# Linear attention and a gated feed-forward layer on one core: other loads first, two chunks' diagonal by TensorE instead of four, first states scaled by VectorE, a new hand-written order

## The chip, the cores and the metric

The kernel runs on 1 core of one Trainium2 chip. The metric is the device time of one launch in microseconds. Engines are called PE (TensorE matmul), PEld (its weight loads), DVE (VectorE), ACT (ScalarE), POOL (GpSimd) and SP (SyncE, which issues the DMAs).

## The reference

```python
for t in range(S):                       # B=4, H=8, S=768, D=48
    kt, vt, rt = k[:, :, t], v[:, :, t], r[:, :, t]
    cur = einsum('bhd,bhe->bhde', u[None] * kt, vt)
    y[:, :, t] = einsum('bhd,bhde->bhe', rt, state + cur)
    state = w[None, :, :, None] * state + einsum('bhd,bhe->bhde', kt, vt)
x = y as [3072 tokens, 384]
h = x @ w_in                             # 384 -> 2048
g = h * erf(softplus(h))
return g @ w_out                         # 2048 -> 384
```

## The kernel before, in words

**Attention.** The sequence is cut into pieces of 128 tokens: 24 chunks, number g = 4 * piece + batch. A block is one piece of all four batches (chunks 4b to 4b+3, 512 tokens); there are 6 blocks. Heads lie in pairs, 48 + 48 rows of 112. One chunk takes these steps, each a word of the order written out at the end of the file: `La`, `Lb` load its two parts; `K`, `R`, `N` scale k, r and k in the other layout by powers of w; `A` (line 290) makes the 128x128 score matrices of both halves; `P` masks them into `am`; `Y` (313) multiplies with v and adds the state's part; `D` (335) makes the chunk's addition to the state; `Sa`, `Sb` add it, `Sc`, `Sd` scale the state by w to the 128th; `Xa`, `Xb` (356, 359) split y into a high and a low part of the feed-forward input x, in the first block with `Xc` (370), in which PE subtracts the high part in PSUM.

**The diagonal** (the term with u) is made in two ways. In the chunks that have a word `G`, DVE or POOL multiplies r and k (`G`, 224), PE sums the product over the head with two columns (`V`, 232), the sums are scaled onto v (`Q`, `diag_v`, 249) and PE adds them with `ident` (the last twelve matmuls of `Y`). `V` also turns k (238) and `N*` copies it back (255). In all other chunks `Qa`, `Qb`, `Qc` (259, 262, 266) multiply and reduce on DVE or POOL, and `M` (277 or 279) lays the sums on a diagonal, onto which `P` (295) copies the scores. Before, chunks 0 to 3 have `G`.

**Feed-forward.** A step n is one block and one of 16 slices of 128 hidden columns. Steps 0 to 7 are slices 0 to 7 of block 0, steps 8 to 15 the same slices of block 1, steps 16 to 23 slices 8 to 15 of block 0, 24 to 31 those of block 1; from step 32 on block after block. `f` is h = x @ w_in (9 matmuls of 512 columns, line 392), then a chain of nine alternating steps on ACT and DVE (`a b z c d e g h l`), then `p` (9 matmuls, 452) into the accumulators. `O` stores: partial sums after steps 7 and 15, results at a block's end.

**Weights** arrive as 64-bit numbers in 16 groups of 768 columns: `F0g` loads group g of w_in, `F1g` of w_out (two buffers), and `C0g`, `C1g` turn each into a high and a low part in six steps a to f: a (ACT, 123), b, c, d (DVE, 125, 127, 130), e (ACT, 133), f (DVE or, with a +, POOL, 135). There is one work buffer `wt`, so a group's step a waits for step f of the group before. Group g of w_in is needed by the steps of slices 2g and 2g+1: `f8` and its block need none that steps 0 to 7 did not, `f16` is the first that needs group C04, and `p20`, `p22` need C16 and C17.

**What sets the order.** Every engine works its own list in the order of the words of `ORDER`, and waits where an operand isn't there yet. A + behind a word puts it on POOL, a * on ACT, else DVE. `W n` puts n dummy matmuls (92) at that place, after 16 at the start. SP issues the loads in the same order; chunks other than 3 share three buffers.

Of the kernel before, what the change touches and what calls it, by code (L numbers as in the profile page):

```python
# [685 lines left out]
C01f W2 f2 N5+ S4a l0 f3 L6a F02 L6b C11a d1 C11b C11c e1 a2 C11d P51 p0x p0y Q7b+ b2 z2 g1 Q7c C11e a3 b3 z3 S4b h1
l1 C11f+ Q6a+ p0z Y5 p1 D5 C02a C02b C02c C02d Q6b Q6c c2 d2 c3 d3 X5a C02e e3 C02f f4 M60+ R6+ K6+ M61+ M70+ M71+ K7+
g3 h3 S5b X5b l3 e2 S5a g2 F13 L8a F12 a4 b4 z4 h2 l2 f5 a5 b5 z5 A6 c4 C13a c5 d5 d4 P60 P61 C13b C13c C13d f6 e5 a6
p2 A7 C13e b6 g5 e4 h5 P70 N7+ C13f+ N6+ C12a p3 P71 Y7 z6 g4 l5 h4 c6 d6 X7a f7 Y6 C12b C12c C12d X7b l4 C12e D6 C12f
p4 a7 F06 L8b b7 z7 e6 X6a c7 C06a d7 X6b f8 D7 g6 C06b C06c p5 h6 C06d Q8a S7b l6 a8 b8 C06e e7 Q8b+ z8 g7 c8 F05 L9a  # L690
# [5 lines left out]
C07d g15 z16 P80 P81 p14 C07e F17 O71b O72b a17 c16 b17 z17 h15 l15 C07f+ N8+ p15x p15y p15z Y8 D8 C05a C05b C05c C05d
c17 d16 d17 e16 e17 C05e O150a g16 h16 g17 C05f f18 l16 f19 p16x O150b C17a O151a h17 O152a a18 b18 C17b C17c C17d z18
C17e c18 l17 C17f d18 e18 O151b F15 C15a O230a O152b L10a O231a L10b F16 p16y p16z f20 g18 h18 C15b l18 a19 b19 a20
C15c z19 C15d b20 z20 c19 d19 C15e e19 C15f g19 f21 a21 p17 b21 z21 h19 l19 C16a c20 d20 e20 C16b C16c g20 C16d p18
p19 f22 c21 h20 d21 l20 e21 C16e g21 C16f a22 b22 z22 h21 c22 d22 e22 X8a l21 S8a X8b f23 a23 b23 g22 Q10a z23 p20 h22  # L700
c23 d23 e23 l22 S8b Q10b Q10c S8d+ R10+ g23 f24 a24 M100+ p21 h23 A9 f25 P90 P91 l23 a25 b25 b24 z25 N9 z24 K10+ c25
d25 e25 c24 d24 S7c+ M101 p22 p23x p23y p23z A10 f26 O230b g25 e24 h25 P100 N10+ g24 h24 a26 Y9 X9a b26 M110+ l25 P101
l24 z26 f27 a27 p24x c26 f28 a28 b28 d26 e26 b27 O231b K11 S6c+ R11 X9b M111 A11 p24y O230c O232a O232b P110 z28 g26
P111 p24z p25 Y11 D11 c28 h26 l26 z27 c27 X11a d27 e27 g27 X11b h27 S11a l27 f29 p26 d28 a29 b29 e28 L12a O231c L12b
z29 S11b g28 c29 d29 h28 Q12a+ Q12b+ S8c+ l28 f30 a30 b30 e29 g29 z30 Q12c M120 Y10 D10 p27 p28 f31 O310a L13a O232c
# [96 lines left out]
```

## Time and profile before

| | |
|---|---|
| three runs | 538.97, 539.66 (median), 540.29 us |
| the profiled execution | 540.45 us, its span 538.6 us |
| PE busy | 518.6 us, 96% of the span |
| ACT, DVE, POOL busy | 393.0 (73%), 354.4 (66%), 126.2 us (23%) |
| chain that ended last | PE 82%, DVE 6%, DMA 4%, ACT 3% |

How to read it: the span is the time between the first and the last instruction on the core, the execution's own time is 1.85 us longer. PE is busy nearly throughout, but a busy PE is not always at full rate: its clock is granted at one of two levels, and the page shows the granted share in 40 slices. A stretch in which PE is busy with dummies, at the lower clock, or waits, is the only place where the time of a fixed amount of matrix work can shrink. The last matmul starts at 532.03 us; what follows is copies and the output's DMA.

### The profile page before, as it was taken

The page shows a single profiled execution, that of the slowest core. Times are in us where ns is not written, and L with a number is a line of the kernel's source. Part 1 is how long each engine was busy: PE and PEld are TensorE (multiplying, and loading weights), DVE is VectorE, ACT ScalarE, POOL GpSimd, SP SyncE. Part 2 cuts the span into 40 slices and gives each one's busy share as a digit, 9 for nine tenths or more (in the row PEclk, how much of TensorE's full clock was granted, in tenths as well). Part 3 has the DMA queues.
Part 4 walks back from the last instruction along what each step waited for, and adds up shares of the span by engine and source line. Part 5 has one row for each costly group of instructions (what it writes and reads, how often), then busy time and mean ns, then how long its engine had stood idle before and what let it go on. Part 6 is the DMA issues. An engine that isn't in the chain of part 4 may idle for free.

```text
span 538.6 us, 9791 instructions
## 1 busy us (share of the span) xinstructions
PE 518.6 (96%) x3893; PEld 409.5 (76%) x3894; DVE 354.4 (66%) x573; ACT 393.0 (73%) x721; POOL 126.2 (23%) x125
## 2 busy tenths in 40 slices
...
PEclk9599999999999999999999999999999999999998
...
GB/s 280 80 271 162 194 108 182 179 112 60 163 236 1 39 105 127 60 211 1 0 1 53 226 1 0 86 1 59 193 106 86 0 1 2 1 60 0 1 1 64
DMA packets 13988, 47.29 MB, mean 88 GB/s; under 512 B 1776, under 2 KB 2416, under 8 KB 13936
## 3 DMA queue, kind: packets, MB, share of 16 engines
...
## 4 chain that ended last, share of the span: by engine, by line
PE 82%; DVE 6%; DMA 4%; ACT 3%; issue 2%; SPq 1%; DVEq 0%; ACTq 0%
PE acc L452 35%; PE h L392 34%; PE y L313 6%; PE A L290 4%; DMA raw<-in_win_dram 3%; PE ds L335 1%; DMA raw<-in_wout_dram 1%; DVE wt L127 1%; ACT wt L123 1%; DVE s L408 1%; DVE wt L125 1%; DVE h L424 1%; DVE wil L135 0%; ACT gh L430 0%; PE y L370 0%
## 5 line engine op out<-in xcount | busy, mean ns | idle before, releaser
L392 PE MATMUL h<-x,wih 128*128 128x512 f32 x576 | 184.2, 401 | 3.1 <-ACT wih L133 2.0
L392 PEld LDWEIGHTS h<-x,wih 128*128 128x128 f32 x576 | 106.5, 188 | 31.4 <-DVE gl L435 3.4
L452 PE MATMUL acc<-gh,woh 128*128 128x512 f32 x288 | 116.4, 404 | 0.0
L452 PE MATMUL acc<-gl,woh 128*128 128x512 f32 x288 | 114.3, 397 | 1.9 <-DVE gl L435 1.9
L392 PE MATMUL h<-x,wil 128*128 128x512 f32 x288 | 114.3, 397 | 0.3 <-DVE wil L135 0.3
L452 PE MATMUL acc<-gh,wol 128*128 128x512 f32 x288 | 114.1, 396 | 0.0
L424 DVE SCALAR_TENSOR_TENSOR h<-s,h 128x512 f32<-128x512 f32 x96 | 66.4, 692 | 63.7 <-ACT s L420 63.5
L408 DVE SCALAR_TENSOR_TENSOR s<-s,h 128x512 f32<-128x512 f32 x96 | 65.5, 682 | 40.6 <-ACT s L403 40.2
L435 DVE TENSOR_TENSOR gl<-h,gh 128x512 fp32r<-128x512 f32 x96 | 66.1, 688 | 35.6 <-ACT gh L430 33.9
L430 ACT CAST gh<-h 128x512 fp32r<-128x512 f32 x96 | 55.9, 582 | 38.1 <-DVE h L424 28.6
L412 ACT ACTIVATE s<-s 128x512 f32<-128x512 f32 x96 | 60.3, 628 | 26.1 <-DVE s L408 26.0
L399 ACT ACTIVATE s<-h 128x512 f32<-128x512 f32 x96 | 56.9, 593 | 27.8 <-PE h L392 27.6
L452 PEld LDWEIGHTS acc<-gh,woh 128*128 128x128 f32 x288 | 54.2, 188 | 15.0 <-issue 1.0
L452 PEld LDWEIGHTS acc<-gl,woh 128*128 128x128 f32 x288 | 54.3, 188 | 14.8 <-DVE gl L435 2.5
L392 PEld LDWEIGHTS h<-x,wil 128*128 128x128 f32 x288 | 54.2, 188 | 14.1 <-DVE wil L135 1.0
L452 PEld LDWEIGHTS acc<-gh,wol 128*128 128x128 f32 x288 | 54.2, 188 | 13.0
L403 ACT ACTIVATE s<-s 128x512 f32<-128x512 f32 x96 | 60.4, 630 | 1.8
L416 ACT ACTIVATE s<-s 128x512 f32<-128x512 f32 x96 | 60.3, 630 | 1.9
L420 ACT ACTIVATE s<-s 128x512 f32<-128x512 f32 x96 | 60.2, 629 | 1.5
L259 POOL TENSOR_TENSOR att<-att,ub 128x384 f32<-128x384 f32 x14 | 16.7, 1190 | 105.1 <-DMA att<-in_att_dram 65.7
L290 PEld LDWEIGHTS A<-att 48*128 48x128 f32 x384 | 24.5, 193 | 10.2 <-issue 6.3
L295 DVE COPY_PREDICATED am<-mask,A 128x512 f32<-128x512 uint32 x40 | 28.1, 736 | 5.7 <-PE A L290 5.7
...
## 6 DMA issues: line engine op xcount, KB each, us to landing
...
```

The costliest lines, as they stand in the source:

```text
L290: nc.tensor.matmul(out=ap[hh][:, p, :], lhsT=t[r, 512 + p * C:512 + (p + 1) * C], rhs=t[r, p * C:(p + 1) * C], start=True, stop=True)
L392: nc.tensor.matmul(out=h, lhsT=w[:, f, q, :], rhs=x[:, xi, q, :], start=k == 0, stop=k == 8)
L399: nc.scalar.activation(out=s1, in_=e["h"], func=AF.Tanh, bias=FB0, scale=FA0)
L403: nc.scalar.activation(out=s1, in_=s1, func=AF.Tanh, bias=FB1, scale=FA1)
L408: nc.vector.scalar_tensor_tensor(out=e["s"], in0=e["s1"], scalar=FG, in1=e["h"], op0=ALU.mult, op1=ALU.add)
L412: nc.scalar.activation(out=s, in_=s, func=AF.Tanh, bias=FB2, scale=FA2)
L416: nc.scalar.activation(out=s, in_=s, func=AF.Square, bias=FB3, scale=FA3)
L420: nc.scalar.activation(out=s, in_=s, func=AF.Square, bias=FB4, scale=FA4)
L424: nc.vector.scalar_tensor_tensor(out=h, in0=ff[n]["s"], scalar=FC, in1=h, op0=ALU.subtract, op1=ALU.mult, reverse0=True)
L430: nc.scalar.copy(out=e["gh"], in_=e["h"])
L435: eng.tensor_tensor(out=e["gl"], in0=e["h"], in1=e["gh"].bitcast(F32), op=ALU.subtract)
L452: nc.tensor.matmul(out=acc[e], lhsT=w[:, f, es], rhs=g, start=first and i == 0, stop=last and i == 2)
```

## The change

- `G2`, `V2`, `Q2` and `G3`, `V3`, `Q3` are gone: chunks 2 and 3 take the other way to the diagonal (`Qa` to `Qc`, `M`, `P` by copy_predicated), and load their second parts whole (608 KB instead of 224 KB each). Their `N` is a product on DVE instead of a turn on PE and a copy on ACT.
- In the four chunks of the first block the scaling of the state by w to the 128th, which the turn of k by `w128` gave, is a DVE product `Sc`, `Sd` (one for each half, 8 in all) instead of an ACT copy. The table `w128` and its POOL product are gone; for chunks 0 and 1 the turn is a plain transpose.
- The last block's copies of accumulators 1 and 2: each whole, by DVE and by ACT, instead of half and half.
- A new `ORDER`, with dummies as nine pairs (18 after the 16 at the start, before 20).

```diff
-    w128 = fp.tile([PR, NPAIR, PR], F32, tag="o", name="w128")
     def diagonals():
         nc.scalar.mul(out=neg, in_=ident, mul=-1.0)
-        nc.gpsimd.tensor_tensor(out=w128, in0=ident[:PR, None, :PR].to_broadcast([PR, NPAIR, PR]),
-                                in1=wp[:, 7, 0, :, None].to_broadcast([PR, NPAIR, PR]), op=ALU.mult)
...
                 kp = chunks[g][:PR, 512 + p * C:512 + (p + 1) * C]
-                if g < 4:
-                    nc.tensor.matmul(out=kt[:, p, :], lhsT=kp, rhs=w128[:, p, :], start=True, stop=True)
-                else:
-                    nc.tensor.transpose(out=kt[:, p, :], in_=kp, identity=ident[:PR, :PR])
+                nc.tensor.transpose(out=kt[:, p, :], in_=kp, identity=ident[:PR, :PR])
...
         if g < 4:
-            nc.scalar.copy(out=sv, in_=ds[r])
+            nc.vector.tensor_tensor(out=sv, in0=ds[r], in1=w128, op=ALU.mult)
...
-            elif b == NB - 1 and e > 0:
-                nc.vector.tensor_copy(out=o[:, 0:TB // 2], in_=full[n, e][:, 0:TB // 2])
-                nc.scalar.copy(out=o[:, TB // 2:TB], in_=full[n, e][:, TB // 2:TB])
+            elif b == NB - 1 and e == 1:
+                nc.vector.tensor_copy(out=o, in_=full[n, e])
...
 ORDER = """
-L1a L1b U0 L0a L2a L0b F00 L3a F03 L3b L2b B0* C00a B0 H0 K1 R0 K0 R1 T0 W5 A0 G0 V0 G1 C00b P00 P01 R3+ V1 C00c R2 Q0
...
+L0a W2 W2 W2 L1a U0 L0b L2a L2b L3a L3b L1b F00 B0 B0* F01 K0 R0 A0 K1 G0 R1 V0 A1 G1 P00 K2+ V1 Q0 P01 P10 T0 H0 N0*
...
```

The weight groups are turned in the order C00, C03, C10, C01, C11, C02, C13, C12, C06, C14, C04, C07, C05, C17, C15, C16 before, and C00, C01, C10, C02, C11, C03, C12, C13, C14, C05, C04, C07, C15, C06, C16, C17 now. Step f of nine groups is POOL's now (C00, C10, C02, C03, C14, C05, C07, C15, C06), before of four (C11, C13, C04, C07). The order of the loads at the start, SP, before (att_160 is chunk 1, att_164 chunk 0, att_166 and att_171 chunks 2 and 3; 128x1024 is the first part, `raw` is weights):

```order
L68 DMA att_160<-in_att_dram 128x1024
L72 DMA att_160<-in_att_dram 128x448
L81 DMA ub<-in_u_dram 128x384
L68 DMA att_164<-in_att_dram 128x1024
L68 DMA att_166<-in_att_dram 128x1024
L72 DMA att_164<-in_att_dram 128x448
L107 DMA raw_169<-in_win_dram 128x768
L68 DMA att_171<-in_att_dram 128x1024
L107 DMA raw_173<-in_win_dram 128x768
L72 DMA att_171<-in_att_dram 128x448
L72 DMA att_166<-in_att_dram 128x448
```

And now (att_159 and att_170 are chunks 0 and 1, att_174 and att_177 chunks 2 and 3):

```order
L68 DMA att_159<-in_att_dram 128x1024
L68 DMA att_170<-in_att_dram 128x1024
L81 DMA ub<-in_u_dram 128x384
L72 DMA att_159<-in_att_dram 128x448
L68 DMA att_174<-in_att_dram 128x1024
L72 DMA att_174<-in_att_dram 128x1216
L68 DMA att_177<-in_att_dram 128x1024
L72 DMA att_177<-in_att_dram 128x1216
L72 DMA att_170<-in_att_dram 128x448
L107 DMA raw_181<-in_win_dram 128x768
L107 DMA raw_187<-in_win_dram 128x768
```

Chunk 0 comes first instead of fourth, and the first weights come last instead of seventh.

DVE in the first block, before, from the first masks of the scores on (kt holds the sums of `V`, wt the weights in work):

```order
L299 TENSOR_TENSOR am_1_224<-A_1_201,mask 128x512
L127 SCALAR_TENSOR_TENSOR wt_179<-raw_169,wt_179 128x768
L215 TENSOR_TENSOR att_166<-att_166,wr 112x512
L249 TENSOR_TENSOR att_164<-att_164,kt_211 128x4x48 x2
L249 TENSOR_TENSOR att_160<-att_160,kt_227 128x4x48 x2
L130 SCALAR_TENSOR_TENSOR wt_179<-raw_169,wt_179 128x768
L299 TENSOR_TENSOR am_0_311<-A_0_256,mask 128x512
L299 TENSOR_TENSOR am_1_313<-A_1_257,mask 128x512
```

And now (its line 253 is 259 of before, 256 is 262, 260 is 266, 293 is 299, 243 is 249, and 341 the new product of the state):

```order
L212 TENSOR_TENSOR att_174<-att_174,wr 112x512
L256 TENSOR_TENSOR att_174<-att_174 128x384
L253 TENSOR_TENSOR att_177<-att_177,ub 128x384
L260 TENSOR_REDUCE q_307<-att_174 128x8
L293 TENSOR_TENSOR am_1_309<-A_1_214,mask 128x512
L243 TENSOR_TENSOR att_170<-att_170,kt_227 128x4x48 x2
L341 TENSOR_TENSOR sbd<-ds_283,wp 48x4x48
L260 TENSOR_REDUCE q_321<-att_177 128x8
L341 TENSOR_TENSOR sbd<-ds_292,wp 48x4x48 x2
L125 TENSOR_SCALAR wt_352<-wt_352 128x768
L216 TENSOR_TENSOR att_177<-att_177,wkn 128x384
L127 SCALAR_TENSOR_TENSOR wt_352<-raw_181,wt_352 128x768
```

The first group's steps stand among the first masks before, and now behind the masks of chunks 0 and 1 and the first two states.

PE from the end of the dummies to the first `Y`, before, without the rows that repeat:

```order
L290 MATMUL A_1_201<-att_164 128x128
L232 MATMUL kt_211<-uw,att_164 128x2 x4
L238 MATMUL kt_211<-w_134,att_164 128x112 x4
L232 MATMUL kt_227<-uw,att_160 128x2 x4
L238 MATMUL kt_227<-w_134,att_160 128x112 x4
L335 MATMUL ds_247<-att_164 48x48 x8
L290 MATMUL A_0_256<-att_160 128x128
L313 MATMUL y_266<-am_0_222,att_164 32x128 x2
```

And now (284 is 290 of before, 229 is 232, 234 is 238, 307 is 313):

```order
L284 MATMUL A_1_192<-att_159 128x128
L229 MATMUL kt_204<-uw,att_159 128x2 x4
L234 MATMUL kt_204<-ident,att_159 128x112 x4
L284 MATMUL A_0_213<-att_170 128x128
L229 MATMUL kt_227<-uw,att_170 128x2 x4
L234 MATMUL kt_227<-ident,att_170 128x112 x4
L192 MATMUL tp<-ident,wk 128x112 x4
L307 MATMUL y_254<-am_0_224,att_159 32x128 x2
```

The first `A` and `V` follow one another as before, but the two `V` are apart, and the first `Y` comes ahead of the first `D`.

## Rows read from the trace of the kernel before

**Rows 1.** The page: its first line, its line of busy times, and of its 40 equal slices the granted TensorE clock in tenths of full speed.

```profile
span 538.6 us, 9791 instructions
PE 518.6 (96%) x3893; PEld 409.5 (76%) x3894; DVE 354.4 (66%) x573; ACT 393.0 (73%) x721; POOL 126.2 (23%) x125
PEclk9599999999999999999999999999999999999998
```

**Rows 2.** The busy time of each engine in four stretches: from the first `f` on, from the end of PE's last early wait to `f8`, from `f8` to the last weight group, and from there to the last matmul (columns: the stretch, its length, then for PE, PEld, DVE, ACT and POOL the busy us with the count of instructions, then the granted clock, the DMA engines' busy share, and GB/s).

```profile
45.20:74.50 29.30, 25.14 (x240) 17.80 (x239) 27.26 (x40) 21.51 (x39) 14.99 (x10) 1.00 0.48 161
74.50:94.00 19.50, 19.50 (x215) 15.25 (x216) 17.10 (x26) 16.27 (x29) 9.23 (x8) 1.00 0.38 128
94.00:165.00 71.00, 70.14 (x384) 55.16 (x383) 60.38 (x87) 64.41 (x110) 23.12 (x20) 1.00 0.42 143
165.00:532.40 367.40, 365.07 (x2592) 289.82 (x2590) 218.79 (x358) 274.90 (x507) 65.36 (x67) 1.00 0.15 52
```

**Rows 3.** What PE's matmuls waited for in the whole span (us in total, times, longest).

```profile
PE h L392 <- ACT wih L133: 2.0, 1, 2.0
PE acc L452 <- DVE gl L435: 1.9, 1, 1.9
```

**Rows 4.** PE in order of time (start us, us, engine, line, operation, tiles, count; in brackets the idle time before it and what ended it): dummies, the first `A`, the first `Y`, the `Y` behind the second pause, the starts of `f0`, `f8`, `p20` and `p22`.

```profile
7.79 1.24 PE L92 MATMUL dummy<-warm 128*128 128x512 bf16 x5
10.84 1.16 PE L290 MATMUL A<-att 48*128 48x128 f32 x16 [1.80 <-DVE att L211]
22.51 1.93 PE L313 MATMUL y<-am,att 128*32 128x128 f32 x32
39.34 1.65 PE L313 MATMUL y<-am,att 128*32 128x128 f32 x26 [1.97 <-DVE am L299]
45.16 0.73 PE L392 MATMUL h<-x,wih 128*128 128x512 f32 x2
93.99 0.63 PE L392 MATMUL h<-x,wih 128*128 128x512 f32 x2
165.23 0.39 PE L452 MATMUL acc<-gh,woh 128*128 128x512 f32 x1
174.97 0.39 PE L452 MATMUL acc<-gh,woh 128*128 128x512 f32 x1
```

**Rows 5.** Three stretches with the granted clock, columns as in rows 2: the first stretch at the lower level, the second, and a pause of PE.

```profile
12.20:25.60 13.40, 13.20 (x120) 12.09 (x120) 8.84 (x13) 3.52 (x9) 6.17 (x4) 0.50 0.29 117
39.40:42.80 3.40, 3.40 (x54) 2.97 (x55) 3.40 (x7) 2.52 (x9) 0.00 (x0) 0.51 0.90 304
69.30:71.20 1.90, 0.00 (x0) 0.00 (x0) 1.86 (x3) 1.34 (x4) 0.22 (x1) 1.00 0.40 60
```

**Rows 6.** The first loads, columns as in rows 2: from 2 us to the arrival of chunk 0, from there to that of the first weights, and the rest.

```profile
2.00:9.40 7.40, 6.67 (x25) 2.63 (x24) 5.11 (x25) 1.02 (x4) 2.90 (x4) 1.00 0.88 287
9.40:13.30 3.90, 2.33 (x22) 2.17 (x22) 3.10 (x5) 0.03 (x1) 0.00 (x0) 0.85 1.03 406
13.30:16.70 3.40, 3.40 (x18) 3.40 (x17) 2.51 (x4) 1.49 (x4) 2.03 (x2) 0.50 0.79 316
```

**Rows 7.** DVE, POOL and ACT in order of time, columns as in rows 4: DVE's first products of a chunk, a product and two small products while POOL works, one of 384 columns, POOL's two products, ACT's first step a.

```profile
7.33 0.69 DVE L211 TENSOR_TENSOR att<-att,wk 112x512 f32<-112x512 f32 x1
9.49 0.69 DVE L215 TENSOR_TENSOR att<-att,wr 112x512 f32<-112x512 f32 x1 [1.47 <-DMA att<-in_att_dram]
10.10 0.68 DVE L211 TENSOR_TENSOR att<-att,wk 112x512 f32<-112x512 f32 x1
16.73 1.76 DVE L215 TENSOR_TENSOR att<-att,wr 112x512 f32<-112x512 f32 x1
18.41 0.60 DVE L249 TENSOR_TENSOR att<-att,kt 128x192 f32<-128x192 f32 x2
44.31 0.55 DVE L259 TENSOR_TENSOR att<-att,ub 128x384 f32<-128x384 f32 x1
15.90 3.71 POOL L211 TENSOR_TENSOR att<-att,wk 112x512 f32<-112x512 f32 x2
13.27 0.89 ACT L123 ACTIVATE wt<-raw 128x768 f32<-128x768 f32 x1 [6.77 <-DMA raw<-in_win_dram]
```

**Rows 8.** Weight groups, columns as in rows 4: step f of C00, step a of C10, step f of C12 and of C16, the last group.

```profile
28.10 0.95 DVE L135 TENSOR_TENSOR wil<-wt,wih 128x768 fp32r<-128x768 f32 x1
42.90 0.91 ACT L123 ACTIVATE wt<-raw 128x768 f32<-128x768 f32 x1
90.66 0.95 DVE L135 TENSOR_TENSOR wol<-wt,woh 128x768 fp32r<-128x768 f32 x1
164.13 0.96 DVE L135 TENSOR_TENSOR wol<-wt,woh 128x768 fp32r<-128x768 f32 x1
```

**Rows 9.** Step f of the weights by DVE and by POOL (groups of instructions: line, engine, operation, tiles, shapes, count, busy us, mean ns, idle time before and what ended it).

```profile
L135 DVE TENSOR_TENSOR wil<-wt,wih 128x768 fp32r<-128x768 f32 x6 | 6.2, 1026 | 0.0
L135 POOL TENSOR_TENSOR wil<-wt,wih 128x768 fp32r<-128x768 f32 x2 | 3.7, 1871 | 10.5 <-ACT wih L133 10.5
```

**Rows 10.** The last copies (accumulator 0's by ACT at 531.06), columns as in rows 4.

```profile
532.46 0.42 DVE L472 COPY o<-acc 128x256 f32<-128x256 f32 x1 [0.28 <-PE acc L452]
531.06 0.59 ACT L475 COPY o<-acc 128x512 f32<-128x512 f32 x1 [2.21 <-PE acc L452]
532.92 0.37 ACT L473 COPY o<-acc 128x256 f32<-128x256 f32 x1 [0.33 <-DVE o L472]
```

More of the change, by code (lines that the diff above doesn't have):

```diff
@@ L686 @@
[L686 to L690, printed above, removed]
@@ L696 @@
[L696 to L700, printed above, removed]
@@ L701 @@
[L701 to L705, printed above, removed]
@@ new lines @@
+C00c W2 X0c C00d N2 K3 X0b X1a C00e M31* D3 A2 X1c A3 X1b P20 P21 Y2 S3c P30 P31 L5a F10 D2 Y3 C00f+ Q4a+ C01a X2a K4
+C01b Q4b C01c K5 C01d S3d Q4c S2d R4+ X3a X2c X3c W2 X2b X3b f0 f1 C01e L6a L5b F02 a0 b0 C01f R5 M40 M41+ A4 S2c z0
+C10a a1 b1 C10b Q5a z1 C10c C10d c0 d0 e0 c1 d1 C10e f2 W2 a2 W2 W2 W2 F11 L6b P40 g0 h0 b2 Q5b+ C10f+ Q5c P41 l0 C02a
+M50* N4+ z2 M51 A5 C02b C02c C02d K6+ c2 f3 d2 a3 e2 e1 C02e p0x p0y p0z P50 g2 h2 b3 Q6a P51 g1 z3 C02f+ Q6b+ R6+ Y4
+X4a D4 h1 c3 X4b l2 Q6c l1 C11a d3 L7a L7b F03 Y5 f4 f5 M60* X5a M61* e3 C11b C11c N5 C11d S4b S4a X5b C11e F12 R7+
@@ new lines @@
+p8z p9 f12 g10 h10 S7a S6a z11 C05b C05c c11 d11 e11 C05d C05e g11 h11 l10 l11 S7b O72b L10a L10b L9a L9b F07 a12 b12
+C05f+ S6b z12 f13 f14 p10 C04a C04b C04c C04d p11 Y8 c12 a13 b13 d12 F15 e12 g12 z13 a14 C04e C04f b14 z14 h12 l12
+C07a f15 p12 c14 c13 d13 e13 d14 C07b C07c C07d g13 C07e h13 e14 a15 Q10a+ Q10b C07f+ F06 l13 g14 b15 z15 h14 l14 C15a
+C15b f16 f17 c15 a16 d15 p13 p14 b16 S5c C15c C15d z16 e15 a17 g15 c16 b17 z17 h15 l15 C15e d16 e16 Q9a+ g16 C15f+
+Q9b+ c17 d17 h16 l16 p15x O150a p15y f18 e17 C06a f19 O151a a18 b18 a19 p15z p16x O150b F16 p16y g17 h17 b19 O152a
@@ new lines @@
+C06b Q9c C06c C06d z18 l17 z19 D8 p16z p17 C06e c18 d18 e18 c19 g18 Q10c d19 h18 l18 e19 O152b O151b F17 O230a O231a
+L11a L11b g19 S8a M90+ C06f+ S5d+ K9+ R10+ f20 f21 a20 h19 l19 f22 b20 z20 C16a p18 c20 d20 e20 a21 a22 b21 p19 C16b
+S8b C16c C16d g20 z21 b22 z22 h20 l20 c21 C16e d21 C16f e21 C17a g21 h21 C17b l21 f23 p20 a23 b23 c22 d22 C17c z23 e22
+c23 p21 f24 g22 h22 d23 C17d l22 e23 g23 C17e C17f h23 l23 a24 b24 X8a z24 R9 X8b S8d+ M91 N9+ M100+ S7c+ S7d+ Q11a+
+Q11b+ N11+ f25 p22 p23x O230b a25 c24 d24 b25 e24 p23y A9 f26 O230c O232a z25 g24 h24 l24 c25 d25 a26 b26 P90 f27 P91
@@ new lines @@
+O231b Y9 z26 K10 Q11c M101+ p23z p24x p24y c26 d26 X9a e26 M110* M111+ S6d+ R11+ S8c+ K11+ S6c+ X9b g26 h26 e25 O232b
+l26 A10 g25 P100 P101 p24z h25 l25 a27 f28 b27 z27 A11 p25 f29 c27 d27 e27 a28 b28 P110 P111 Y11 D11 z28 g27 c28 d28
+h27 l27 a29 X11a e28 b29 g28 S11a X11b p26 f30 h28 z29 l28 c29 d29 e29 a30 b30 S11b z30 f31 a31 c30 Y10 D9 p27 O231c
+O232c L12a L12b O310a O311a L13a L13b d30 b31 e30 p28 R12 g29 g30 h30 X10a Q12a+ Q12b+ l30 X10b h29 S9a l29 z31 f32
+p29 f33 a32 b32 z32 c31 c32 d31 Q12c e31 M120* K12+ S9b Q13a+ g31 h31 M121 A12 N12 S11d+ K13+ S11c+ Q13b+ S9c+ p30 d32
@@ new lines @@
+l31 e32 g32 h32 a33 b33 p31x O310b Q13c M130+ N10+ l32 p31y f34 f35 P120 P121 z33 O311b Y12 D10 p31z p32x a34 b34 c33
+z34 a35 c34 d33 e33 g33 d34 h33 b35 O310c O312a O312b l33 z35 p32y p32z e34 c35 X12a g34 d35 e35 h34 p33 f36 g35 h35
+l34 S10b l35 a36 b36 z36 S10a O311c L14a f37 c36 a37 p34 D12 f38 p35 L14b L15a O312c L15b b37 d36 S12a z37 Q14a+ e36
+c37 Q14b+ g36 h36 a38 X12b S12b l36 b38 d37 e37 g37 z38 h37 c38 l37 Q14c f39 p36 f40 a39 d38 e38 g38 h38 N13+ R13+
+N14+ M131* b39 l38 z39 A13 p37 a40 c39 b40 d39 e39 Q15a+ Q15b+ S9d+ P130 P131 z40 g39 c40 h39 l39 f41 d40 p38 p39 f42
@@ new lines @@
+K17+ S15d+ f49 p46 p47x p47y p47z A16 f50 a49 b49 z49 c48 d48 e48 S14c+ g48 Q18a K18 c49 h48 d49 l48 f51 e49 O470a
+L17b O470b g49 h49 O471a a50 b50 Q17a R17+ P160 l49 z50 a51 c50 d50 O472a f52 p48x p48y p48z b51 Q17b Q17c S12c z51
+P161 e50 c51 g50 h50 l50 Q18b Q18c M170* N18 N17 M171+ p49 A17 a52 d51 e51 b52 g51 z52 h51 P170 l51 p50 f53 a53 b53
+c52 d52 P171 z53 Y16 Y17 p51 f54 c53 e52 g52 d53 h52 e53 M180+ R18+ M181* g53 l52 h53 l53 a54 X16a X17a b54 X17b X16b
+z54 p52 f55 f56 A18 p53 c54 d54 e54 g54 h54 l54 a56 a55 b55 b56 z55 z56 P180 N16+ S14d+ p54 D16 f57 c55 c56 d56 e56
@@ new lines @@
+S16b g56 P181 Y18 d55 e55 S16a g55 h55 l55 a57 h56 b57 l56 z57 D18 f58 f59 p55 X18a c57 d57 a58 e57 b58 S18b O472b
+O471b L19a L19b X18b K19 g57 z58 c58 d58 h57 S18a l57 p56 p57 e58 g58 a59 h58 b59 Q19a+ R19+ l58 Q19b z59 Q19c c59 d59
+M190+ e59 M191+ f60 A19 f61 g59 P190 P191 Y19 N19 D19 h59 a60 b60 z60 l59 p58 f62 c60 a61 d60 e60 X19a b61 z61 g60
+X19b h60 c61 d61 l60 L20a L20b D17 L22a a62 b62 z62 e61 g61 Q20a p59 f63 h61 c62 Q20b+ l61 d62 a63 b63 e62 p60 L22b
+L21a L21b p61 f64 K21 S19b S16d+ S19d+ K22 g62 h62 S19a z63 Q20c M200+ K20+ c63 d63 l62 S17a e63 a64 b64 S17b g63 h63
```

74 lines of the change are left out of this document (27 added, 47 removed).

## The prediction, made before the changed kernel was run

> **What bounds the kernel now.** I read the page first: the span, and PE busy for 96% of it [rows 1]. That says that PE's list is the path, and that only three things can be gained: time in which PE waits, time in which it runs dummies, and time at the lower clock. So I looked for them by stretch. From 165 us to the last matmul PE is busy for 365.07 of 367.40 us, from 74.5 to 165 for all but 0.9 [rows 2]; the list of what PE waited for holds one wait of 1.9 us behind 94 us and else only early ones [rows 3]. What can be gained lies in the first 94 us. PE's rows there show it: first `Y` at 22.51, `f0` at 45.16, `f8` only at 93.99 [rows 4], and the granted clock was at its lower level, 1.2 GHz, from 12.2 to 25.6 us and again for 3.4 us, with PE busy, after pauses of PE of 1.80 and 1.97 us (they stand in brackets, and ended at 10.84 and 39.34) [rows 4, 5].
>
> Why PE pauses after `f0`: the weight groups pass one work buffer, one behind the other. From the end of C00's step f (28.10 + 0.95 = 29.05) to the end of C16's, the last, (165.09) 15 groups took 136.0 us, 9.07 each; the six from C10 to C12 took 48.7, 8.1 each [rows 8]. `p20`, which needs C16, started at 165.23 [rows 4], just behind it. So two chains matter up to `p22`: PE's list, and the weight groups.
>
> **The change, part by part.**
>
> *First loads.* Chunk 0 was fourth in the queue, 1.47 MB with what stands ahead of it, and DVE had it at 9.49; by 9.4 us 7.4 x 287 GB/s = 2.12 MB had moved. The first weights end at 3.01 MB in the queue and came at 13.27, when 3.7 MB had moved [rows 6, 7]. A load thus lands when some 0.65 to 0.7 MB more have moved than lie up to its end. Now chunk 0 is first and takes the place of the load that was there by 7.33 without a wait. Chunk 1 (1.05 MB) lands by some 8.0, chunk 3's second part (3.77 MB) at 15.1, F00 (4.78 MB, 5.48 to be moved: 13.3 + 1.77 MB / 406 GB/s) at 17.7 instead of 13.27. Chunks 2 and 3 bring 0.79 MB more, some 2 us at that rate, all of it ahead of F00. That is the price of the new order of loads, and it falls on weights.
>
> *PE's start.* 22 dummies, one more than now but with no transposes between them, end as now at about 7.79 + 1.24 = 9.0 [rows 4]; `K0` and `R0` need two steps of 0.61 from 7.33 [rows 7], 8.55. `A0` follows at 9.0 without the pause of 1.80. I take it that the clock then stays up, since what brought it down here followed a pause. `A0`, `V0`, `A1`, `V1` and the transposes (1.1 + 1.6 + 1.1 + 1.6 + 0.6) end at 15.0; `Y0` starts there, 7.5 earlier.
>
> *DVE in the first block.* Gone are two `G` on DVE or POOL, four small `Q`, eight ACT copies of states; new are six steps of 384 columns, two of them on POOL, two `N` on DVE, eight state products of 0.3, the `M` on POOL and ACT. Up to C00's step b the list holds 11 steps of 512 columns at 0.61, 4 of 384 at 0.48, 8 small ones at 0.30 [rows 7]: 11.0 us, from 7.33 to 18.3, with waits for chunk 3's load 19.2. Steps b, c, d with one `N` between end at 22.2, e at 23.0, f by POOL 1.87 [rows 9] at 24.9. The rest of the block on DVE (`N2`, `K3`, four `P`, one S) ends at 26.4; with `Y3`, two `Xc` and the last copies `f0` starts at about 29 instead of 45.2. PE loses some 7 us of `V` and ident work, part of it at the lower clock; it is part of these 16 us and isn't counted again.
>
> *Where these 16 us go.* Not all reach the end, since the weight chain sets `p22`. C00 is done at 24.9 instead of 29.05, but it is followed by C01 at once, where before C10 started only at 42.90 behind C03. Six groups more, with C12 the last of them, at 48.7: 73.6. Behind it DVE has C13's three steps and two z before the last part of x for block 1 (4.2), so `f8` is at 78 to 79, 15 earlier. From `f8` to `p22` PE has one `p` and one `A` less and one `D` more (2.8 us less than the 81.0 of now), so PE alone would reach `p22` at 157. The chain needs 24.9 + 136.0 = 161, since C17 is again the fifteenth group behind C00 and the DVE work up to there is the same within 1.1 us. I take 161, the later. Before it was 174.97 [rows 4]. PE waits some 4 us in between.
>
> *The rest.* Behind `p22` PE has 357.45 us up to 532.42, and in the new order one `A` more, 1.2. The waits of 1.9 and 0.4 may go or others come; I leave them. In the tail, accumulator 2's copy is 0.42 + 0.04 + 0.37 on two engines one after the other [rows 10], now one on ACT like accumulator 0's, 0.59 [rows 10]: 0.24 less. The other half copy runs beside matmuls and counts nothing.
>
> *Sum.* 161 + 357.45 + 1.2 + 6.18 - 0.24 = 525.6 of span against 538.6 [rows 1]. The execution took 1.85 more than its span, and stood 0.8 above the median of the runs: **about 526.6 us**, 13 less.
>
> *Bounds.* Below: DVE's list alone sets `f8`. Counted with its rows' durations it has 64.1 us of work up to there, behind 7.2 of tables: 71.3. If PE then never waits, `p22` is at 149.5 (78.2 later), and with the wait of 1.9 gone the time is 513. Above: five more groups have step f on POOL, 1.87 instead of 1.03 [rows 9], 4.2 in all, and the low clock of rows 5 comes back (next part), 6.7: 538. I take the measured pace, since as many DVE steps stand between the groups as before.
>
> *A rule against it.* DVE's product of 512 columns at 16.73 took 1.76 instead of 0.69, while POOL ran two products; the small ones that read PSUM took 0.30 as ever [rows 7]. The Trainium skill (SBUF — State Buffer, "SBUF: two separate sides") says why: DVE with two operands in SBUF and POOL take one port pair in turn, for a whole instruction. The trace agrees. By the rule each microsecond that the new order gives POOL may be taken from DVE: POOL has 30.8 us up to `f8`, counted with its rows' durations, and 28.1 before. If all 2.7 were lost by DVE, the sum would be 529.3 instead of 526.6.
>
> **Rivals.**
>
> *The clock falls again in the new start.* For it: from 12.2 to 25.6 PE was busy for 13.20 of 13.40 us and stayed at the lower level all the same, with `V` and `A`, which the new start has too [rows 5]; against it: from 25.6 to 39 it ran the same kinds of work at the upper level. Price: half of 13.4, 6.7 us on the way to `f0` and C00's steps, which wait for the first states: 533. The Trainium skill (TensorE: Matmul & The Clock Gate, "What's actually happening") has the lower level as the default, which activity releases; by that the pauses between weight groups could bring it back too. The pause at 69.3 to 71.2, 1.9 us long, did not [rows 5].
>
> *The gain at the start is taken back by the weights.* If ACT or POOL makes the groups slower than 9.07, it is lost. ACT is busy for 64.41 of 71.0 us from `f8` to C16 [rows 2]; by the same counting the new order has 78.7 us of ACT work from `f8` to `p22`, in a stretch that I make 82 long. At 10.0 us a group C17 ends at 175 and nothing is won: 540. That is no change.
>
> *Slower.* The same chain, past that point: with 10.4 us a group C17 ends at 181, `p22` waits for it, and the time is 546. It decides from 10.0 on. For it: POOL has nine steps f instead of four, three of them while DVE has the most to do, and later loads of weights wait for buffers in one queue behind loads of chunks. Against it: no stretch of 15 groups was above 9.1 here.
>
> *The order doesn't do what it says.* F00 could land later than 17.7, if the larger chunk loads take more than their bytes. Each microsecond there moves C00, not the first block: 2 to 3 at the most, 529.
>
> **How the numbers follow.** A measurement of this kernel can tell some 0.2%, 1.1 us, from no change. My forecast, a gain of 9 to 14 us or more with the chain at its old pace, has 0.62; the clock 0.14; late loads 0.06; a partial loss to no change 0.10, of which 0.04 within 1.1 us; slower 0.08. Faster by over 0.2%: 0.62 + 0.14 + 0.06 + 0.06 = 0.88; within: 0.04; slower: 0.08. The range reaches from the lower bound to the case in which nothing is won: 513 to 540.
>
> **What would show it.** Right: first `Y` near 15, `f0` near 29, C00's f near 25, `f8` near 79, `p22` near 161, granted clock at the upper level from 5 us on, PE dense behind `p22`. Wrong: a granted clock of 0.5 before `f0`; groups above 9.5 us; new waits of PE behind 165 us above 3 us in sum; a wait for loads of `raw`.

## The result and the profile of the changed kernel

The changed kernel took 525.79 us (median of 4 runs, 524.04 to 527.54), the kernel before 539.97 (4 runs, 538.97 to 541.41): ratio 0.9735, 95% interval 0.9695 to 0.9775. A later repeat gave 526.5 (6 runs, 523.78 to 528.94), ratio 0.9765 (0.9733 to 0.9797). The prediction was 526.6.

The profiled execution took 524.04 us, the shortest of its four; traces are therefore compared span with span: 538.6 and 522.3, 16.3 us apart. That is 2.1 more than the 14.2 between the medians; the account below is one of these two executions. The page, as [rows 1]:

```profile
span 522.3 us, 9636 instructions
PE 506.9 (97%) x3804; PEld 398.0 (76%) x3804; DVE 352.5 (67%) x572; ACT 393.0 (75%) x720; POOL 142.7 (27%) x135
PEclk9998999999999999999999999999999999999999
```

PE is busy for 11.7 us less and does nothing for 4.6 us less; work at the lower clock counts as busy for as long as it takes. The places on PE's list, as [rows 4]; line 284 is 290 of before, 307 is 313, 386 is 392, 446 is 452:

```profile
2.37 7.12 PE L92 MATMUL dummy<-warm 128*128 128x512 bf16 x22 [2.37 <-ACT warm L86]
9.42 1.16 PE L284 MATMUL A<-att 48*128 48x128 f32 x16
14.84 1.08 PE L307 MATMUL y<-am,att 128*32 128x128 f32 x32
28.35 0.97 PE L386 MATMUL h<-x,wih 128*128 128x512 f32 x2
41.19 1.16 PE L284 MATMUL A<-att 48*128 48x128 f32 x14 [1.20 <-DVE am L289]
77.35 0.51 PE L446 MATMUL acc<-gh,wol 128*128 128x512 f32 x1 [0.75 <-DVE wol L135]
81.20 0.77 PE L386 MATMUL h<-x,wih 128*128 128x512 f32 x2
158.07 0.39 PE L446 MATMUL acc<-gh,woh 128*128 128x512 f32 x1
516.14 0.39 PE L446 MATMUL acc<-gh,wol 128*128 128x512 f32 x1
```

The first `A` has no pause ahead of it, `f0` starts at 28.35 instead of 45.16, `f8` at 81.20 instead of 93.99, `p22` at 158.07 instead of 174.97, the last matmul at 516.14 instead of 532.03. The stretches between them (columns as in [rows 2]):

```profile
20.00:28.35 8.35, 7.95 (x146) 6.50 (x145) 8.28 (x15) 5.55 (x13) 5.40 (x3) 1.00 0.78 268
28.35:43.00 14.65, 12.66 (x72) 8.46 (x71) 14.47 (x24) 11.31 (x19) 7.90 (x6) 1.00 0.54 188
43.00:46.80 3.80, 3.80 (x12) 2.97 (x11) 3.73 (x5) 2.80 (x7) 1.22 (x1) 0.55 0.23 92
47.00:81.20 34.20, 31.95 (x375) 24.82 (x374) 33.48 (x47) 27.34 (x54) 20.39 (x15) 1.00 0.45 161
81.20:158.00 76.80, 76.80 (x427) 60.69 (x426) 65.86 (x96) 72.21 (x125) 31.04 (x24) 1.00 0.41 145
158.00:516.60 358.60, 356.61 (x2555) 283.07 (x2554) 210.36 (x343) 265.43 (x486) 68.01 (x70) 1.00 0.15 53
```

Read DVE's column, the third behind the length: from 20 us to `f8` it is busy for 98 to 99% of every stretch. In the kernel before it was not, ahead of `f0`:

```profile
20.00:45.16 25.16, 23.19 (x395) 20.26 (x391) 16.43 (x25) 11.02 (x29) 4.14 (x4) 0.82 0.59 202
45.16:94.00 48.84, 44.67 (x454) 33.09 (x454) 44.40 (x65) 37.83 (x68) 24.21 (x17) 1.00 0.44 148
```

So the account of the 16.3 us is: `f0` 16.81 earlier; 52.85 us from `f0` to `f8` instead of 48.83, 4.02 given back (some 2.8 of it, by estimate, one `p` and one `A` less a `D`, which before stood behind `f8`); from `f8` to the last matmul 434.94 instead of 438.04, 3.10 gained, most of it that same work; behind it 6.16 instead of 6.57, 0.41 gained.

On PE's side the 16.81 us up to `f0` are 24.90 us of busy time instead of 38.69 and 3.45 idle instead of 6.47. Of the 13.8 less busy some 8.3 are, by estimate, the clock: before, 16.6 us of PE's work there ran at half rate [rows 5], and in this execution none did. The rest is matmuls that are gone or stand elsewhere.

The last copies, as [rows 10]:

```profile
515.86 0.69 DVE L465 COPY o<-acc 128x512 f32<-128x512 f32 x1 [2.20 <-PE acc L446]
516.57 0.58 ACT L467 COPY o<-acc 128x512 f32<-128x512 f32 x1 [0.82 <-PE acc L446]
```

The last one ends 0.62 us behind the last matmul (516.53) instead of 0.87.

### The profile page after: what moved, and what is told of

The parts are those of the page before. It is cut to its first block, busy times and chain, and to the rows that moved or that the text cites. A ratio compares the mean times of both kernels' runs of the same rounds, so it can differ in the third digit from the quotient of the medians.

```text
span 522.3 us, 9636 instructions
## 1 busy us (share of the span) xinstructions
PE 506.9 (97%) x3804; PEld 398.0 (76%) x3804; DVE 352.5 (67%) x572; ACT 393.0 (75%) x720; POOL 142.7 (27%) x135
## 4 chain that ended last, share of the span: by engine, by line
PE 87%; DVE 9%; issue 1%; ACT 1%; POOL 0%; DVEq 0%; ACTq 0%; POOLq 0%
PE acc L446 38%; PE h L386 36%; PE y L307 6%; PE A L284 4%; PE ds L329 1%; PE dummy L92 1%; DVE wt L127 1%; DVE am L289 1%; DVE wt L130 1%; DVE wol L135 1%; DVE wt L125 1%; DVE gl L429 1%; DVE s L402 0%; DVE q L260 0%; DVE att L212 0%
## 5 line engine op out<-in xcount | busy, mean ns | idle before, releaser
L273 POOL TENSOR_TENSOR am<-ident,q 128x512 f32<-128x512 f32 x24 | 27.8, 1166 | 96.2 <-DVE q L260 48.4
L289 DVE COPY_PREDICATED am<-mask,A 128x512 f32<-128x512 uint32 x44 | 31.0, 733 | 2.0 <-PE A L284 1.9
```

## The experiments

Starts of `f0` and `f8` and the span belong to the profiled execution, the time is the median of all runs, the ratio is to the kernel before on the same chip.

| kernel | `f0` | `f8` | span | span less `f0` | time | ratio, 95% interval |
|---|---|---|---|---|---|---|
| before | 45.16 | 93.99 | 538.6 | 493.4 | 539.97 | |
| changed | 28.35 | 81.20 | 522.3 | 494.0 | 525.79 | 0.9735 (0.9695 to 0.9775) |
| changed, again | 28.30 | 81.16 | 522.1 | 493.8 | 526.50 | 0.9765 (0.9733 to 0.9797) |
| old, chunk 0 first | 44.23 | 91.94 | 538.5 | 494.3 | 539.11 | 0.9994 (0.9966 to 1.0022) |
| the same, dummies in the pause | 43.80 | 91.59 | 537.3 | 493.5 | 538.18 | 0.9965 (0.9947 to 0.9984) |
| new, chunk 1 first | 33.83 | 87.81 | 529.0 | 495.2 | 532.10 | 0.9881 (0.9846 to 0.9916) |
| new, diagonal by PE, first places | 38.29 | 90.81 | 532.1 | 493.8 | 534.73 | 0.9921 (0.9902 to 0.9940) |
| new, diagonal by PE, better places | 31.76 | 84.54 | 525.6 | 493.8 | 529.09 | 0.9831 (0.9788 to 0.9874) |
| new, three parts undone | 37.07 | 89.48 | 532.1 | 495.0 | 534.64 | 0.9925 (0.9897 to 0.9954) |
| new, without seven steps c | 30.58 | 78.92 | 519.9 | 489.3 | 519.68 | 0.9636 (0.9619 to 0.9653) |
| new, two work buffers | 31.28 | 85.90 | 527.2 | 495.9 | 527.75 | 0.9766 (0.9730 to 0.9802) |
| new, f of C11, C12 by POOL | 31.26 | 82.23 | 525.6 | 494.3 | 526.50 | 0.9757 (0.9729 to 0.9785) |
| the same, Xb first | 28.41 | 80.42 | 526.7 | 498.3 | 530.53 | 0.9810 (0.9780 to 0.9840) |
| new, 16 dummies | 29.33 | 83.52 | 524.5 | 495.2 | 525.52 | 0.9719 (0.9689 to 0.9748) |

The column of the span less `f0` is the finding: where only the start was altered it stays between 493.4 and 495.2 us, old order or new. Whatever `f0` gains or loses arrives at the end, within these 1.8 us.

**The first load alone, in the old order.**

```diff
-L1a L1b U0 L0a L2a L0b F00 ... H0 K1 R0 K0 R1 T0 W5 A0
+L0a L1a U0 L0b L2a L1b F00 ... H0 K0 R0 K1 R1 T0 W5 A0
```

> The kernel before, with one thing changed: chunk 0's two parts are loaded ahead of chunk 1's, and DVE scales k and r of chunk 0 first. The rest of the old order stays. Theory (the gain of the change starts with the first load, and what follows PE's first pause is the low clock): the first A starts at 9 to 9.5 instead of 10.84, the granted clock stays at its upper level up to 25 us, the first Y is at 16 to 18 instead of 22.5, f0 at 36 to 39 instead of 45.16; the old list of DVE and the weight groups take some of it back, so that the time is 531 to 535 (540 before). Rival 1 (the clock alone is the whole gain): 526 to 528. Rival 2 (DVE's list of the first block bounds f0 whatever PE does): f0 within 2 us of 45.16, 538 to 540.

It moved nothing: 539.11 us, the interval holds 1. The theory failed here. PE's first pause is gone, and the clock fell all the same, in the next one. PE of this kernel, then the stretch at the lower clock:

```profile
9.95 1.16 PE L290 MATMUL A<-att 48*128 48x128 f32 x16
14.68 1.86 PE L232 MATMUL kt<-uw,att 112*128 112x2 f32 x8 [1.60 <-DVE am L299]
21.79 1.93 PE L313 MATMUL y<-am,att 128*32 128x128 f32 x32
44.23 0.73 PE L392 MATMUL h<-x,wih 128*128 128x512 f32 x2
```

```profile
14.30:24.60 10.30, 9.60 (x104) 8.77 (x104) 7.74 (x11) 2.00 (x5) 5.82 (x4) 0.51 0.15 57
```

The wait is for the masks of chunk 0 (line 299). In DVE's old list a step of the weights stands ahead of them, and that waits for ACT's step a (13.47, then the masks):

```profile
13.47 0.56 DVE L125 TENSOR_SCALAR wt<-wt 128x768 int32<-128x768 int32 x1 [2.43 <-ACT wt L123]
13.94 1.28 DVE L299 TENSOR_TENSOR am<-A,mask 128x512 int32<-128x512 int32 x2
```

**The same with dummies in that pause.**

```diff
-R3+ V1 C00c
+R3+ W7 V1 C00c
```

> The kernel before with chunk 0 loaded first, and seven dummies in PE's list ahead of V1, where it stood 1.60 us at 14.68, the pause behind which the granted clock was at its lower level from 14.5 to 24.7. Theory (the pause brought the clock down): the clock stays at its upper level from 9 to 25 us, first Y at 18 instead of 21.79, f0 3 to 5 us earlier than 44.23, and 1 to 4 us of it in the time: 535 to 538. Rival (the clock falls there in any case, as in a run of the changed kernel at 15 us without a pause; or DVE's list sets f0): f0 within 1 us of 44.23, 538 to 540.

0.35% under before, by its interval a gain, but not the expected one: `f0` moved by 0.4 us against the run above, and both numbers are the rival's. The clock stayed up as far as PE had work, and fell at 17.2, in the pause that came next, 3 us later than without the dummies:

```profile
14.32 0.95 PE L232 MATMUL kt<-uw,att 112*128 112x2 f32 x8
18.11 1.09 PE L335 MATMUL ds<-att 128*48 128x48 f32 x16 [1.85 <-ACT att L255]
```

```profile
12.80:17.20 4.40, 3.45 (x25) 2.53 (x23) 4.40 (x6) 0.56 (x3) 3.84 (x3) 1.00 0.56 222
17.20:24.80 7.60, 6.70 (x96) 5.80 (x98) 3.14 (x7) 2.38 (x6) 2.99 (x2) 0.55 0.01 2
```

ACT's copy of k (line 255) waits for DVE's small products, which stand behind another step of the weights. The old list makes PE pause in several places; to fill one or to load earlier only moves to the next. What the clock alone is worth in the old order stays open: it was down here for 7.6 us, above for 10.3 and before for 13.4, but no run kept it up.

**Chunk 1 first, in the new order.**

```diff
-L0a W2 W2 W2 L1a U0 L0b L2a L2b L3a L3b L1b F00
+L1a W2 W2 W2 L1b U0 L0a L2a L0b L2b L3a L3b F00
```

> The changed kernel, with one thing undone: chunk 1's two parts are loaded first, chunk 0's behind them, as before the change. Theory: DVE waits for chunk 0 to about 9.5, A0 starts at 11 behind a pause of PE, the granted clock falls to its lower level for some 10 us, first Y at 19 to 22 instead of 14.84, f0 at 32 to 35 instead of 28.35; f8 loses less than f0 does, 2 to 4 us, and so the end: 528 to 530. Rival (the weight chain and DVE set f8, and the start of PE has slack): f8 within 1 us of 81.2, 525 to 527.

Here the order of loads counts: `f0` 5.5 us later as expected, and all of it in the time, 532.10, 5.6 to 6.3 above the changed kernel's two medians (528 to 530 was expected). "f8 loses less than f0 does" was wrong; it lost 6.6. DVE waits 2.60 us for chunk 0, PE 1.14, and the clock is down from 14.2 to 21.7, which at half rate is by estimate 3.8 us of the 5.5:

```profile
9.11 0.69 DVE L208 TENSOR_TENSOR att<-att,wk 112x512 f32<-112x512 f32 x1 [2.60 <-DMA att<-in_att_dram]
```

```profile
12.83 1.02 PE L229 MATMUL kt<-uw,att 112*128 112x2 f32 x8 [1.14 <-DVE att L221]
19.28 1.94 PE L307 MATMUL y<-am,att 128*32 128x128 f32 x32
```

```profile
14.20:21.70 7.50, 7.50 (x85) 6.81 (x88) 6.15 (x13) 1.94 (x8) 2.95 (x3) 0.54 0.48 198
```

**The diagonal of chunks 2 and 3 by TensorE again**, twice, since the words had to be put somewhere:

```diff
 first places
-Y0 D0 D1 Q2a+ R2 Q2b Q3a Q3b+ R3+ Q2c P11 M20+ Q1 M21* S0d Q3c Y1 C00a X0a M30* ... C00b N3 C00c W2 X0c C00d N2 K3 X0b X1a C00e M31* D3 A2
+Y0 D0 D1 R2 R3+ G2+ P11 Q1 S0d V2 Y1 C00a X0a N2* ... S1c Q2 S1d C00b K3 C00c W2 X0c C00d G3 V3 X0b X1a C00e N3* Q3 D3 A2
 better places
+Y0 D0 D1 R2 R3+ G2+ K3 P11 G3+ Q1 S0d V2 Y1 C00a X0a N2* ... S1c Q2 S1d V3 N3* C00b Q3 C00c W2 X0c C00d X0b X1a C00e D3 A2
```

> The changed kernel, with the diagonal of chunks 2 and 3 by TensorE again (G, V, Q, a turn of k on PE and its copy on ACT, 24 more matmuls in Y; their second loads 224 KB instead of 608 KB). Theory (the gain is made by loads and order, the way of the diagonal is a small part): PE has 2 x 1.6 us of V and 2 x 0.8 us of ident work more, DVE some 2 us less; f0 at 30 to 33 instead of 28.35, f8 up to 2 us later than 81.2, 526 to 529. Rival (the other way to the diagonal is where the gain came from): f0 at 36 or later, 532 or more.

> As the run with the diagonal of chunks 2 and 3 by TensorE in the new order, but with better places: K3 and G3 (on POOL) two groups of steps earlier, V3 ahead of the weights' step b, so that PE does not wait 3.01 us for G3 behind step d of C00. Theory (what cost 8.9 us there was the pause and the low clock behind it more than the way of the diagonal): f0 at 31 to 34, no stretch at the lower clock before it, 527 to 530. Rival (the diagonal by TensorE itself costs it, in PE's 7 us and the copies on ACT): f0 at 36 to 38, 532 to 535.

The first gave the rival's numbers, 534.73, by a wait of my own making: G3 stood on DVE behind step d of C00, and PE stood still for it, then ran 6.8 us at half rate.

```profile
24.82 1.02 PE L229 MATMUL kt<-uw,att 112*128 112x2 f32 x8 [3.01 <-DVE att L221]
```

```profile
27.00:33.80 6.80, 6.80 (x73) 6.06 (x77) 3.22 (x7) 1.27 (x2) 2.00 (x2) 0.50 0.09 39
```

With K3 and G3 earlier that wait is gone, no stretch ahead of `f0` is at the lower clock, `f0` is at 31.76 and the time 529.09. So the other way to the diagonal is worth 2.6 to 3.3 us against these places of the words; the interval of its ratio just touches that of the repeat, and its `f0`, 3.4 us later, points the same way. The other 5.6 of the first run were the places of a few words.

**Three parts undone together** (the two of above, and the last copies half and half).

> The changed kernel with three parts undone together: chunk 1's loads first (alone 532.10 us), the diagonal of chunks 2 and 3 by TensorE in the better places (alone 529.09), and the last copies of accumulators 1 and 2 half and half. What stays of the change is its order of DVE's work and of the weight groups, the state's products and the dummies. Theory (each part works on the same list of DVE ahead of f8 and they add): 6 + 3 over the changed kernel, 534 to 537, f0 at 36 to 39; in the tail the last copy ends 0.25 us later behind the last matmul than in the changed kernel. Rival 1 (loads and diagonal are the whole gain, the order gives nothing): 538 to 540. Rival 2 (the later of the two sets f0, the other hides behind it): 531 to 533, f0 at 33 to 35.

534.64, `f0` at 37.07: within the scatter the parts add. What is left of the change, the order of DVE's work and of the weights with the states' products and the dummies, is worth 4 to 5 us against before (2.5 to 5.6 by the interval). No run takes these apart. In the tail the pair of copies is back, and ends 0.87 us behind the last matmul:

```profile
524.84 0.42 DVE L465 COPY o<-acc 128x256 f32<-128x256 f32 x1 [0.28 <-PE acc L446]
525.30 0.37 ACT L466 COPY o<-acc 128x256 f32<-128x256 f32 x1 [0.33 <-DVE o L465]
```

**DVE's list up to `f8`.**

```diff
-C00c C01c C10c C02c C11c C03c C12c
```

> The changed kernel without step c of the seven weight groups ahead of f8 (C00, C01, C10, C02, C11, C03, C12): it leaves out the low bits of these weights. DVE has 7 instructions less, 0.96 us each and up to 1.9 beside POOL, 8.4 in all. Theory (DVE's list with the weight chain bounds f8): C12's step f ends 5 to 8 us earlier than 77.30, PE's waits between 28 and 81 us (4.2) shrink, f8 at 76 to 78 instead of 81.2, 520 to 523. Rival (PE's own list with its dummies bounds f8): f8 within 1 us of 81.2, 525 to 527.

In the main as the theory has it: `f0` to `f8` in 48.34 us instead of 52.85, though `f0` itself was 2.2 us later in the profiled execution; 519.68 us. C12's step f ended at 75.02, 2.3 us earlier and not 5 to 8; counted from `f0` it was 4.5. PE's waits between `f0` and `f8` fell to half, 2.07 us instead of 4.24, and the clock did not fall there, which by estimate is another 1.9 of the 4.5. DVE was then still busy for 46.01 of the 48.34 (columns as in [rows 2]):

```profile
30.58:78.92 48.34, 46.27 (x456) 34.80 (x455) 46.01 (x67) 41.35 (x79) 25.67 (x20) 1.00 0.50 179
```

**Two work buffers.**

```diff
-WG, RAWB, WTB = 768, 2, 1
+WG, RAWB, WTB = 768, 2, 2
```

> The changed kernel with two work buffers for the weights instead of one, so that a group's step a no longer waits for step f of the group before. What the prediction said (the chain of groups through one buffer sets f8 and p22): C12's step f 3 us earlier or more, f8 at 78 or earlier, the time 522 to 523.5. Theory now (DVE's busy list sets f8, PE's own list what lies behind it): C17's step f earlier by several us perhaps, f8 within 1 us and the time within 1 us of the changed kernel.

527.75, not faster: in the new order the one buffer, on which the prediction's weight chain rested, is not what sets the groups' pace. With the second one C12's step f ended at 82.01, 50.73 us behind `f0` (48.95 in the changed kernel):

```profile
80.99 1.02 DVE L135 TENSOR_TENSOR wol<-wt,woh 128x768 fp32r<-128x768 f32 x1
```

`f8` at 85.90 missed the 1 us of my theory too: `f0` was 2.9 us later in this execution, and the clock fell once more, from 62.9 to 66.6 us, by estimate 1.9.

**Relief for DVE: two steps f on POOL, then Xb earlier too.**

```diff
-C11f g3 Q7a+ K7+ Q7b+ ... a7 b7 C12f z6
+C11f+ g3 Q7a+ K7+ Q7b+ ... a7 b7 C12f+ z6
 and then
-X7a d7 e6 C13b C13c C13d X7b g6
+X7a d7 e6 X7b C13b C13c C13d g6
```

> The changed kernel with step f of C11 and of C12 on POOL instead of DVE. They stand in POOL's list ahead of products for chunks 7 and 8 that now run beside DVE's steps of the weights (DVE's 1.78 at 57.79, 1.94 at 70.55, 1.66 at 72.52, 1.98 at 75.32, instead of 0.96). Theory (DVE's list, slowed beside POOL, bounds f8): DVE is rid of 3.8 us, C12's step f ends at 75 to 76.5 instead of 77.30, f8 is 1 to 2 us earlier against the run of the changed kernel, 524 to 525. Rival (POOL's 1.85 for each step takes from DVE what it gives, and PE's own list bounds f8): within 0.5 us of the changed kernel or slower.

> The changed kernel with step f of C11 and C12 on POOL, as before, and the low part of x of chunk 7 (Xb, DVE) ahead of C13's steps b, c, d instead of behind them: there PE stood 2.07 us at 84.71, in the middle of f8, for that part of x, which waited behind the three steps of 1.7 us each. Theory (DVE's list bounds f8): f8 begins at 82.2 (with dummies that end at 10.8; 79.3 with 9.45) and goes on without a wait, 1.5 to 2 us less than the changed kernel on the same chip: 524 to 525. Rival (C13 comes later by as much and PE waits for its weights at p5 to p7): no gain, 526 to 527.

Neither is faster. The first took 526.50 us, as the repeat on the same chip, which is the rival's number. In it, C12's step f ended 46.9 us behind `f0` instead of 48.95 and `f8` began 50.97 behind it instead of 52.85, as hoped, but then PE stood 2.07 us in the middle of `f8`, for Xb behind three steps of C13 that POOL's moved products had made slow (0.55, 0.96 and 0.96 elsewhere). PE, DVE and one of POOL's products:

```profile
84.71 0.51 PE L386 MATMUL h<-x,wih 128*128 128x512 f32 x1 [2.07 <-DVE x L353]
```

```profile
79.14 1.69 DVE L125 TENSOR_SCALAR wt<-wt 128x768 int32<-128x768 int32 x1 [0.79 <-ACT wt L123]
80.86 1.66 DVE L127 SCALAR_TENSOR_TENSOR wt<-raw,wt 128x768 int32<-128x768 int32 x1
82.55 1.64 DVE L130 SCALAR_TENSOR_TENSOR wt<-raw,wt 128x768 int32<-128x768 int32 x1
84.11 0.55 DVE L353 TENSOR_TENSOR x<-y,x 128x384 fp32r<-128x384 f32 x1
```

```profile
80.35 1.35 POOL L253 TENSOR_TENSOR att<-att,ub 128x384 f32<-128x384 f32 x1
```

With Xb ahead of them, `f8` ran through, and `f9` waited 3.60 us for the `gl` behind the same three steps; the clock fell behind that wait, from 87.5 to 90.8. The time was 530.53, by the ratios 2.4 to 4.0 us above the changed kernel, and in neither range. My expectation had looked at `f8` alone.

```profile
86.30 0.72 PE L386 MATMUL h<-x,wih 128*128 128x512 f32 x2 [3.60 <-DVE gl L429]
```

**Fewer dummies, and the repeat.**

```diff
-L0a W2 W2 W2 L1a
+L0a L1a
```

> The changed kernel without the three pairs of dummies behind the first 16. DVE has the operands of the first A at 7.9, the 22 dummies end at 9.5 or 10.8. Theory (the dummies only hold PE back, and DVE has slack of 0.2 to 1.5 us there): A0 at 7.9 to 8.7, f0 0.2 to 1.3 us earlier, the time 525 to 526.5 and less scatter. Rival (the six dummies keep PE at the upper level: without them the granted clock falls between 10 and 20 us in all runs): f0 at 31 or later in the profile, 527 to 530.

> The changed kernel once more, unaltered, beside the next three on one chip, for the scatter: 525 to 527, the first A at 9.4 to 10.8 (in the run of the changed kernel without step c its 22 dummies ended 1.3 us later than in the first one), the granted clock at its lower level for some 3 us once or twice before 50 us.

525.52 without the six dummies, in the scatter of the changed kernel (the intervals of the ratios overlap): `A0` at 7.94, but `f0` at 29.33. The rival's fall of the clock between 10 and 20 us did not come in the profiled execution, and the scatter did not shrink (523.43 to 527.73 us). Neither side is shown. No kernel tried here that does the whole of the work is clearly faster than the changed one.

## Why the prediction was right, and where it was not

*The start.* Right: `A0` at 9.42 without a pause (9.0 predicted), first `Y` 14.84 (15.0), C00's step f at 24.77 (24.9), `f0` 28.35 (29). The 11.0 us of DVE rows plus waits were the right thing to count, since in the new order DVE hardly waits. What the steps before it gave as reason was too simple. The first load is not the cause by itself: alone, in the old order, it gave nothing that the time shows, and what the clock alone gives there no run shows. In the new order the first load, with the clock that falls without it, is worth 5.6 to 6.3, the diagonal 2.6 to 3.3, the rest of the order 4 to 5. My reading is that the load counts there because DVE's new list has the masks of chunks 0 and 1 and the first states ahead of the weights; no run puts only these masks back, so that is argued and not shown. In the old list PE and DVE waited for each other in turn, DVE idle for 8.7 of the 25.2 us ahead of `f0`.

*"Not all reach the end, since the weight chain sets p22."* This step failed. `p22` came at 158.07, not 161; PE was busy for all of the 76.80 us up to 158 and the 4 us of waiting did not come. The chain was faster than the 9.07 us a group that I had carried over: from C00's step f to the end of C17's, 132.7 us, 8.84 each. It ended 0.6 us ahead of `p22`:

```profile
156.48 0.96 DVE L135 TENSOR_TENSOR wol<-wt,woh 128x768 fp32r<-128x768 f32 x1
```

From the end of C13's step f to that of C17's it took 72.4 us in ten profiled executions of the new order, with `f8` anywhere from 78.9 to 90.8 and with one buffer or two (73.9 in the eleventh, the one with Xb first). With two buffers, too, C17's step f ended 0.6 us ahead of `p22` (162.15 and 162.78). So the 9.07 of before was no limit of the chain, and a second buffer gains nothing; that the groups behind `f8` keep the pace at which PE hands work to ACT and DVE is my reading of it.

The estimate from PE alone, 157, was the better one, in part by luck: `f8` came 2 to 3 us later than I had put it, and PE took 76.9 us from there to `p22` instead of 78.2.

*Six groups in 48.7 us* failed the other way: C12's step f ended at 77.30, not 73.6, and `f8` came at 81.20 instead of 78 to 79. Two rows of it:

```profile
70.55 1.94 DVE L127 SCALAR_TENSOR_TENSOR wt<-raw,wt 128x768 int32<-128x768 int32 x1
75.32 1.98 DVE L135 TENSOR_TENSOR wol<-wt,woh 128x768 fp32r<-128x768 f32 x1
```

```profile
70.06 1.62 POOL L208 TENSOR_TENSOR att<-att,wk 112x512 f32<-112x512 f32 x1
75.48 1.00 POOL L216 TENSOR_TENSOR att<-att,wkn 128x384 f32<-128x384 f32 x1
```

Both of DVE's take 0.96 elsewhere; POOL was at such products then. Up to `f8` the 27 steps b, c, d, f on DVE took 29.51 us, 6.9 more than at 0.55, 0.96, 0.96 and 0.95; before it was 4.6, in 31 steps. That is 2.3 more, near the 2.7 that the prediction gave for the POOL work that it had counted; some 1.4 of the 3.7 by which C12 was late stay open. The Trainium skill (SBUF — State Buffer, "SBUF: two separate sides") has DVE and POOL take one port pair in turn. The trace agrees, also in that DVE's work on PSUM beside POOL took its 0.7 as ever. The one that waits need not be DVE: beside DVE's steps of 0.95 at 27.40 and 28.87 one of POOL's products took 5.30, which at 16.45 had taken 1.28:

```profile
25.69 5.30 POOL L212 TENSOR_TENSOR att<-att,wr 112x512 f32<-112x512 f32 x1
```

*The rest.* From `p22` to the last matmul's end 358.46 us against 358.65 predicted; the tail's copies 0.25 against 0.24. Behind 165 us two waits remain, 0.98 and 0.84, in place of 1.9 and 0.4.

*The sum.* It gave 525.6 of span, and the profiled span was 522.3: 3.3 too much, 2.9 of it the chain. The median of the runs lies 1.75 above the profiled execution, where I had put it 0.8 below; the nearness of 526.6 to 525.79 is half luck.

*The rivals.* The clock did fall, at 43 to 46.8 behind the pauses that end at 41.19, which at half rate costs some 1.9 us; in other executions (below) also at 15 to 18.8, with no pause ahead of it. That it stayed up to `f0` in the changed kernel's two profiles is thus not a matter of the missing pause alone, as the prediction took it to be. An average of 10 us a group, which would have cost the gain, came in no run: the slowest from C00 to C17 was 9.35, with the diagonal by PE in the first places.
